# Three 768x768 projections under a max, computed as one level of Strassen's algorithm

## The chip, the cores and the metric

The kernel runs on one core of a Trainium2 chip. The metric is device time in microseconds (us) of one execution, as the median of several runs. PE is the matrix engine (PEld its weight load), DVE the vector engine, ACT the scalar engine, POOL the general-purpose engine, and SP the engine whose queue issues every DMA here.

## The reference

Attention for 2 batches of 12 heads (448 positions, head size 64) with capped scores, a first feed-forward block with a rational activation, and a second one whose hidden layer is the largest of three projections:

```python
attn_out = softmax(cap * tanh(q @ k.T / 8 / cap)) @ v          # 2 x 12 x 448 x 64
x = attn_out.transpose(0, 2, 1, 3).reshape(896, 768)
h = x @ w_in                                                    # 896 x 2048
g = (a0 + a1*h + a2*h*h + a3*h**3) / (1 + |b0|*|h| + |b1|*h*h + 1e-6)
y = g @ w_out                                                   # 896 x 768
m = max(max(y @ w1, y @ w2), y @ w3)                            # three 768 x 768 weights: the change is here
out = m @ w_out2                                                # 896 x 768
```

The weights arrive as 64-bit floats. Every large product is made of three matmuls in single precision with rounded operands (fp32r): a value is split into a rounded high part and the rest as a low part, and high x high, high x low and low x high are summed in PSUM.

## The kernel before

**Layout.** Features lie on the 128 partitions and tokens in the free dimension, one batch (448 tokens) at a time. `y` is six slices of 128 features, each with its two batches; a branch weight is 6 x 6 blocks of 128 x 128. There are 51 SBUF slots of 128 x 2 x 448 fp32 (`NSLOT`) for nearly all data: a weight's decoded form, its high part and its low part take a slot each, and so does a high and low pair of an activation for 448 tokens. There are 3 buffers for raw weights, 4 row buffers, and 8 PSUM banks.

**Stages.** Attention, then `up` (the first product) mixed with the first half of `down` (line 756), which makes three slices of `y` for both batches in six accumulator banks (`acc`); then the second half of `down`, which makes the other three slices in six banks again; then the branches; then `output` (line 904). `finish_x2` (line 783) splits an accumulator of `y` into high and low, negated as the activation leaves it: a copy on ACT and a subtraction on DVE.

**Branches.** `branches(oc, b)` runs for 6 slices of output features and 2 batches. For each of the three weights it adds up 6 x 3 = 18 matmuls of 128 x 448 in a bank. ACT or DVE copies the first bank out (L874), DVE takes the maximum with the second (L879) and the third (L884), ACT rounds the result to the high part (L889), and DVE subtracts for the low part (L894). In all 6 x 2 x 3 x 18 = 648 matmuls.

**Weights.** `weight` (line 391) serves one 128 x 768 stripe: a DMA of 768 KB into a raw buffer, a scaling on ACT or POOL (`scale`, L400, L402), a shift on DVE (L406), `rest`, the lowest bits, on DVE (L425) or ACT (L422), `sign` on DVE (L415), then the high part as a copy on ACT or DVE (L441) and the low part as a subtraction on DVE or POOL (L430). The 18 stripes of the three branch weights are `decm`, `whm` and `wlm` in the trace, those of the second half of `w_out` `decob`, `whob`, `wlob`, and the 6 stripes of `w_out2` `deco`, `who`, `wlo`.

**Who decides the order.** The kernel hands operations with cost estimates to a planner, `Flow` (lines 71 to 283), which plays the program through on its own clock and writes out a fixed order for each engine. PE operations are due in the order in which they are added; every other operation is due early enough for those that need it, and an engine takes the ready operation with the earliest due time whose slots, rows and banks are free. An operation with several engines goes to the first named, unless that is so far behind that another ends sooner. Operations marked `shared` are never put on DVE while POOL works, and POOL takes one only if DVE has enough other work meanwhile. `ahead` and `leave` limit how early slots are taken for weights: the scaling must leave 4 slots free, the high part is made at most 40 us ahead.

Of the kernel before, what the change touches and what calls it, by code (L numbers as in the profile page):

```python
# [18 lines left out]
P = 128  # L19
# [266 lines left out]
def f32(ap):  # L286
    return ap.bitcast(F32)
# [3 lines left out]
def attention_moe(ctx: ExitStack, tc: tile.TileContext, qk, v, w_in, w_out, w123, w_out2, par, out):  # L291
# [96 lines left out]

    weights = {}

    def weight(key, src):
        w = weights[key] = Weight()
        kn = "".join(str(x) for x in key)
        raw, dec, lo, hi = Val("raw", f"raw{kn}"), slot(f"dec{kn}"), slot(f"wl{kn}", F32R), slot(f"wh{kn}", F32R)
        w.hi, w.lo = hi, lo
# [13 lines left out]

        def sign(e):
            t = flat(dec).bitcast(I32)
            mask = -0x80000000 if s3.on == "dve" else -0x7FFFFFF9
            dve.scalar_tensor_tensor(  # L415
                out=t, in0=raws[raw.at[0]][:, :, 1], scalar=mask, in1=t, op0=ALU.bitwise_and, op1=ALU.bitwise_or
            )

        def rest(e):
            if e == "act":  # L420
                byte = raws[raw.at[0]].bitcast(U8).rearrange("p n t -> p (n t)")
                act.activation(byte[:, 4::8], byte[:, 3::8], AF.Copy, scale=1 / 32, bias=-31 / 64)  # L422
# [6 lines left out]
        def low(e):  # L429
            engine[e].tensor_tensor(out=flat(lo), in0=flat(dec), in1=f32(flat(hi)), op=ALU.subtract)  # L430
# [9 lines left out]
        s5 = add(  # L440
            {"act": 0.74, "dve": 0.47}, lambda e: copy_on[e](flat(hi), flat(dec)), [s4], [dec, hi],  # L441
            shared=True, leave=KEEP, ahead=LATE,
        )
        w.done = add({"dve": 0.88, "pool": 1.8}, low, [s5], [dec, lo, hi], shared=True)

    def w_hl(w):
        return flat(w.hi), flat(w.lo)
# [16 lines left out]
        weight(("oa", j), w_out[0, j])  # L464
    for j in range(NFC // 2):
        weight(("ob", j), w_out[1, j])
    for oc in range(NCC):
        for m in range(3):
            weight(("m", oc, m), w123[oc, m])
    for oc in range(NCC):  # L470
        weight(("o2", oc), w_out2[oc])

# [283 lines left out]
    def down(which, n, half):  # L756
# [4 lines left out]
        for o in range(3):  # L761
# [14 lines left out]

            users.append(add({"pe": 3 * MM}, products, [w.done, h_, l_], [a, w.hi, w.lo, hi, lo]))
            if half and len(users) == 1:
                X2[b, o][1].before(users[0])

    X2 = {}

    def finish_x2(b, o):
        half, oo = divmod(o, 3)
        a, users = acc[half, oo, b]
        x = slot(f"x2{b}_{o}", F32R)
# [10 lines left out]
        h_ = add({"act": 0.43}, high, users, [a, x])  # L797
        X2[b, o] = x, add({"dve": 0.54}, low, [h_], [a, x])


    for d in range(B * ND):
# [21 lines left out]
    for k in range(NK):  # L823
# [3 lines left out]
            up(2 * (k + LAG) + 1)  # L827
        down("oa", 2 * k, 0)
        down("oa", 2 * k + 1, 0)
    for b in range(B):  # L830
        for o in range(3):
            finish_x2(b, o)
    for k in range(NK):
        down("ob", 2 * k, 1)
        down("ob", 2 * k + 1, 1)
    for b in range(B):
        for o in range(3):
            finish_x2(b, 3 + o)


    H3 = [(slot(f"h3h{oc}", F32R), slot(f"h3l{oc}", F32R), []) for oc in range(NCC)]

    evac = []

    def branches(oc, b):
        outs, deps = [], []
        for m in range(3):
            o = Val("h", f"m{oc}_{b}_{m}")
            outs.append(o)
        ranges = ((0, 3), (3, 6)) if (oc, b) == (0, 0) else ((0, 6),)  # L850
        last = [None] * 3
        for lo, hi in ranges:
            for m in range(3):
                w, o = weights["m", oc, m], outs[m]

                def products(e, w=w, o=o, lo=lo, hi=hi):
                    whl = w_hl(w)
                    for cc in range(lo, hi):
                        x = two(X2[b, cc][0])
                        for i, (w_, x_) in enumerate(three(whl, slice(cc * P, cc * P + P), (x[:, 0], x[:, 1]))):  # L860
                            pe.matmul(bank(o)[:, :S], w_, x_, start=cc == 0 and i == 0, stop=cc == NCC - 1 and i == 2)  # L861

                xs = [X2[b, cc] for cc in range(lo, hi)]
                last[m] = add(
                    {"pe": 3 * MM * (hi - lo)}, products, [w.done, last[m]] + [x[1] for x in xs],
                    [o, w.hi, w.lo] + [x[0] for x in xs],
                )
        if len(evac) > 1:
            evac[-2].before(*last)
        t = slot(f"t{oc}_{b}")  # L870
        hi, lo, dones = H3[oc]
        cols = slice(b * S, b * S + S)
        c0 = add(
            {"act": 0.43, "dve": 0.54}, lambda e: copy_on[e](two(t)[:, 0], bank(outs[0])[:, :S]), [last[0]],  # L874
            [outs[0], t],
        )
        c1 = add(
            {"dve": 0.54},
            lambda e: dve.tensor_tensor(out=two(t)[:, 1], in0=bank(outs[1])[:, :S], in1=two(t)[:, 0], op=ALU.max),  # L879
            [last[1], c0], [outs[1], t],  # L880
        )
        c2 = add(
            {"dve": 0.54},
            lambda e: dve.tensor_tensor(out=two(t)[:, 0], in0=bank(outs[2])[:, :S], in1=two(t)[:, 1], op=ALU.max),  # L884
            [last[2], c1], [outs[2], t],
        )
        evac.append(c2)
        c3 = add(
            {"act": 0.47, "dve": 0.30}, lambda e: copy_on[e](flat(hi, NT)[:, cols], two(t)[:, 0]), [c2],  # L889
            [t, hi], shared=True,  # L890
        )
        dones.append(add(
            {"dve": 0.54, "pool": 1.1},
            lambda e: engine[e].tensor_tensor(  # L894
                out=flat(lo, NT)[:, cols], in0=two(t)[:, 0], in1=f32(flat(hi, NT)[:, cols]), op=ALU.subtract
            ),
            [c3], [t, hi, lo], shared=True,
        ))

    for oc in range(NCC):  # L900
        for b in range(B):
            branches(oc, b)

    def output(t):
        tk = slice(t * P, t * P + P)
# [4 lines left out]
        for half in range(2):  # L910
            o = Val("h", f"o{t}_{half}")
            ck = slice(half * NH, half * NH + NH)

            def products(e, o=o, ck=ck):
                terms = []
                for oc in range(NCC):
                    hi, lo = (flat(H3[oc][z], NT)[:, tk] for z in range(2))
                    wh, wl = w_hl(weights["o2", oc])
                    terms += [(hi, wh[:, ck]), (hi, wl[:, ck]), (lo, wh[:, ck])]
                for i, (h_, w_) in enumerate(terms):  # L920
                    pe.matmul(bank(o)[:, :NH], h_, w_, start=i == 0, stop=i == len(terms) - 1)  # L921

            ws = [weights["o2", oc] for oc in range(NCC)]
            done = add(
                {"pe": 18 * MO}, products, [w.done for w in ws] + [h[2][b] for h in H3 for b in halves],
                [o] + [x for w in ws for x in (w.hi, w.lo)] + [x for h in H3 for x in h[:2]],
            )
# [64 lines left out]
```

## Time and profile before

| | |
|---|---|
| median of 3 runs | 521.94 us (521.74 to 524.34) |
| profiled execution: its time, its span | 524.37 us, 522.6 us |
| PE busy | 510.7 us (98%), 2637 matmuls |
| DVE busy | 358.8 us (69%) |
| ACT busy | 295.1 us (56%) |
| POOL busy | 47.4 us (9%) |

The shares are means over the whole span; the stages differ. Times in the rows below are us from the start of the span unless marked ns. Neighbouring matmuls overlap in the records, as do neighbouring DVE instructions, so the pace of a run is read from the starts and not from the durations.

### The profile page before, as it was taken

The page shows a single profiled execution, that of the slowest core. Times are in us where ns is not written, and L with a number is a line of the kernel's source. Part 1 is how long each engine was busy: PE and PEld are TensorE (multiplying, and loading weights), DVE is VectorE, ACT ScalarE, POOL GpSimd, SP SyncE. Part 2 cuts the span into 40 slices and gives each one's busy share as a digit, 9 for nine tenths or more (in the row PEclk, how much of TensorE's full clock was granted, in tenths as well). Part 3 has the DMA queues.
Part 4 walks back from the last instruction along what each step waited for, and adds up shares of the span by engine and source line. Part 5 has one row for each costly group of instructions (what it writes and reads, how often), then busy time and mean ns, then how long its engine had stood idle before and what let it go on. Part 6 is the DMA issues. An engine that isn't in the chain of part 4 may idle for free.

```text
span 522.6 us, 6706 instructions
## 1 busy us (share of the span) xinstructions
PE 510.7 (98%) x2637; PEld 418.0 (80%) x2637; DVE 358.8 (69%) x494; ACT 295.1 (56%) x407; POOL 47.4 (9%) x48
## 2 busy tenths in 40 slices
PE   8899999997999999999999999999999999999997
PEld 5333333676899889999997999999999999999996
DVE  0267999989999998788899999999842417111000
ACT  6999999956778866466766553474621121101111
POOL 0202303001201120101010200100000000000000
PEclk9999999999899999999999999999999999999999
DMA  8956755344101112000013678768400000000211
GB/s 308 365 181 217 243 180 212 111 156 154 62 0 61 60 61 60 1 1 2 1 61 99 217 251 279 249 210 271 176 0 2 0 1 0 1 0 10 80 64 61
DMA packets 16448, 58.37 MB, mean 112 GB/s; under 512 B 3592, under 2 KB 6944, under 8 KB 16416
## 3 DMA queue, kind: packets, MB, share of 16 engines
q1 hardware_dynamic: 16416, 57.94, 32.4%
q8 instruction: 20, 0.33, 0.3%
q14 instruction: 12, 0.10, 0.1%
HBM read 55.10 MB, written 2.84 MB: 111 GB/s over the span
## 4 chain that ended last, share of the span: by engine, by line
PE 60%; DVE 18%; DMA 9%; ACT 8%; issue 2%; SPq 2%; DVEq 0%; ACTq 0%
PE b L861 25%; PE b L773 16%; PE b L666 11%; PE b L921 8%; ACT e L536 4%; DMA rsum<-comp 3%; ACT e L539 3%; DMA row<-rsum 3%; SPq L343 2%; DVE W L697 2%; DMA comp<-sums 2%; DVE W L700 2%; DVE W L728 2%; DVE T L725 2%; DVE W L731 1%
## 5 line engine op out<-in xcount | busy, mean ns | idle before, releaser
L861 PE MATMUL b<-x,whm 128*128 128x448 f32 x432 | 122.6, 365 | 0.0
L666 PE MATMUL b<-x,whin 128*128 128x448 f32 x384 | 112.4, 373 | 2.7 <-DVE x L646 1.4
L861 PEld LDWEIGHTS b<-x,whm 128*128 128x128 f32 x432 | 81.1, 188 | 6.4
L666 PEld LDWEIGHTS b<-x,whin 128*128 128x128 f32 x384 | 72.4, 190 | 14.2 <-issue 3.0
L861 PE MATMUL b<-x,wlm 128*128 128x448 f32 x216 | 78.9, 365 | 0.0
L666 PE MATMUL b<-x,wlin 128*128 128x448 f32 x192 | 71.2, 371 | 0.0
L536 ACT ACTIVATE e<-b,qscale 128x448 f32<-128x448 f32 x84 | 49.0, 811 | 2.3 <-PE b L515 2.3
L889 ACT CAST h3h<-t 128x448 fp32r<-128x448 f32 x12 | 6.8, 567 | 66.8 <-DVE t L884 66.7
L539 ACT ACTIVATE e<-e,con 128x896 f32<-128x896 f32 x42 | 44.3, 1249 | 0.0
L861 PEld LDWEIGHTS b<-x,wlm 128*128 128x128 f32 x216 | 40.6, 188 | 3.2
L666 PEld LDWEIGHTS b<-x,wlin 128*128 128x128 f32 x192 | 36.5, 190 | 3.6
L773 PE MATMUL b<-gl,whoa 128*128 128x448 f32 x96 | 35.5, 369 | 2.2 <-DVE gl L748 2.2
L773 PE MATMUL b<-gh,wloa 128*128 128x448 f32 x96 | 35.2, 367 | 0.0
L773 PE MATMUL b<-gh,whoa 128*128 128x448 f32 x96 | 35.2, 367 | 0.0
L773 PE MATMUL b<-gh,whob 128*128 128x448 f32 x96 | 35.2, 366 | 0.0
L515 PE MATMUL b<-qk 64*128 64x448 f32 x144 | 33.6, 564 | 1.6 <-ACT e L536 1.4
L773 PE MATMUL b<-gh,wlob 128*128 128x448 f32 x96 | 35.1, 365 | 0.0
L773 PE MATMUL b<-gl,whob 128*128 128x448 f32 x96 | 35.1, 365 | 0.0
L686 ACT ACTIVATE W<-b,con 128x448 f32<-128x448 f32 x32 | 23.0, 719 | 18.6 <-PE b L666 18.5
L879 DVE TENSOR_TENSOR t<-b,t 128x448 f32<-128x448 f32 x12 | 7.5, 622 | 33.9 <-PE b L861 33.8
L515 PEld LDWEIGHTS b<-qk 64*128 64x128 f32 x144 | 14.3, 186 | 20.1 <-ACT e L536 9.5
L575 PE MATMUL b<-e,v 128*64 128x448 f32 x144 | 29.0, 545 | 0.0
(111 smaller groups left out, 917.7 us busy)
## 6 DMA issues: line engine op xcount, KB each, us to landing
raw<-in_w_out_dram SPq DMA_DIRECT2D x22, 768.0 KB, 4.4
raw<-in_w_dram SPq DMA_DIRECT2D x18, 768.0 KB, 4.2
raw<-in_w_in_dram SPq DMA_DIRECT2D x16, 768.0 KB, 6.0
qk<-in_qk_dram SPq DMA_DIRECT2D x12, 448.0 KB, 7.7
v<-in_v_dram SPq DMA_DIRECT2D x6, 448.0 KB, 11.9
row<-rsum SPq DMA_DIRECT2D x24, 112.0 KB, 3.6
out_dram<-ob SPq DMA_DIRECT2D x6, 384.0 KB, 2.8
out_dram<-ob SPq DMA_DIRECT2D x2, 192.0 KB, 1.9
```

Source lines behind the costliest of these rows:

```text
L343: return add({"sp": issue}, lambda e: nc.sync.dma_start(out=out_(), in_=in_()), after, vals, size=size, **kw)
L515: pe.matmul(pair(t, j)[:, :S], k[rr], q[rr], start=True, stop=True)
L536: act.activation(two(x)[:, j], pair(t, j)[:, :S], AF.Tanh, scale=qscale)
L539: act.activation(two(x), two(x), AF.Exp, scale=cap)
L575: pe.matmul(bank(o)[j * D : j * D + D, :S], whole(vr, n, r, j), two(x)[:, j], start=False, stop=n == NFULL - 1,)
L666: pe.matmul(bank(h)[:, :S], w_, x_, start=cc == 0 and i == 0, stop=cc == NCC - 1 and i == len(terms) - 1)
L686: act.activation(two(w_)[:, i], bank(h)[:, :S], AF.Identity, bias=a2, scale=a3)
L697: dve.tensor_tensor(out=two(w_)[:, i], in0=bank(h)[:, :S], in1=two(w_)[:, i], op=ALU.mult)
L700: dve.scalar_tensor_tensor(out=two(w_)[:, i], in0=two(w_)[:, i], scalar=a1, in1=bank(h)[:, :S], op0=ALU.add, op1=ALU.mult)
L773: pe.matmul(bank(a)[:, :S], w_, g_, start=count[half, o, b] == 1, stop=count[half, o, b] == 3 * NFC)
L861: pe.matmul(bank(o)[:, :S], w_, x_, start=cc == 0 and i == 0, stop=cc == NCC - 1 and i == 2)
L921: pe.matmul(bank(o)[:, :NH], h_, w_, start=i == 0, stop=i == len(terms) - 1)
```

## The change

The branch weights, the `y` of both batches and the result are each seen as 2 x 2 blocks: output features 0-383 and 384-767, contraction halves 0-383 and 384-767, and the two batches. Seven half-size products per weight replace eight (Winograd's form of Strassen's algorithm). `o` = 0, 1, 2 stands for the output slices `o` and `o` + 3, and with 3 weights (`m`) there are 9 sets; a set has 7 products of 3 x 3 = 9 matmuls of 128 x 448, so 567 matmuls in all. Sums of weight blocks are formed before the split into high and low, and sums of products after, in fp32.

`branch_weights` decodes two stripes (`top`, `bot`), combines their halves with four 384-wide additions or subtractions, and splits three and a half stripes in place of two: a set then occupies seven slots (`h1`, `l1`, `h2`, `l2`, `h3`, `l3`, `x4`). `finish_near` and `finish_far` make seven split operands for each of 3 feature slices (`B11`, `T1`, then `T2`, `T3`, `T4`, `B21`, `B22`) out of the accumulators, where there were four. `branches(n)` adds seven banks into four corners with `put`; the maximum is then taken in SBUF (`most`) for the second and third weight. The first two products of the first two sets need only the near half and are put first. For the first two token tiles `output` is cut into two pieces, output slices 0, 1, 3, 4 and then 2, 5.

```diff
@@ weight() is cut into decoded() (up to sign), split() and weight(); the steps of decoded() are unchanged
+    def split(dec, at, n, hi, hat, lo, lat, after):
+        def high(e):
+            copy_on[e](flat(hi)[:, hat : hat + n], flat(dec)[:, at : at + n])
+        def low(e):
+            engine[e].tensor_tensor(
+                out=flat(lo)[:, lat : lat + n], in0=flat(dec)[:, at : at + n], in1=f32(flat(hi)[:, hat : hat + n]),
+                op=ALU.subtract,
+            )
+        f = n / DM
+        s5 = add({"act": 0.1 + 0.64 * f, "dve": 0.07 + 0.4 * f}, high, after, [dec, hi], shared=True, leave=KEEP, ahead=LATE)
+        return add({"dve": 0.06 + 0.82 * f, "pool": 0.1 + 1.7 * f}, low, [s5], [dec, lo, hi], shared=True)
...
+    def branch_weights(o, m):
...
+        def combine(out_, x, y, op, after):
+            (o_, oc), (x_, xc), (y_, yc) = out_, x, y
+            return add(
+                {"dve": 0.47, "pool": 0.95},
+                lambda e: engine[e].tensor_tensor(out=flat(o_)[:, oc], in0=flat(x_)[:, xc], in1=flat(y_)[:, yc], op=op),
+                after, [o_, x_, y_], shared=True,
+            )
...
+        s1 = combine((sd, first), (bot, first), (bot, second), ALU.add, [b4])
+        s2 = combine((sd, second), (sd, first), (top, first), ALU.subtract, [s1, t4])
+        s3 = combine((bot, first), (top, first), (bot, first), ALU.subtract, [s1, t4])
+        d1 = split(top, 0, DM, h1, 0, l1, 0, [t4])
+        d3 = split(sd, 0, DM, h3, 0, l3, 0, [s1, s2])
+        d2 = split(bot, 0, DM, h2, 0, l2, 0, [s3])
+        s4 = combine((top, second), (top, second), (sd, second), ALU.subtract, [d1, s2])
+        d4 = split(top, NH, NH, x4, 0, x4, NH, [s4])
...
-    for oc in range(NCC):
+    for o in range(3):
         for m in range(3):
-            weight(("m", oc, m), w123[oc, m])
+            branch_weights(o, m)
...
+    def from_bank(name, o, a, after):       # as finish_x2: high on ACT, low on DVE, both out of PSUM
...
+    def from_slot(name, o, t, i, after):
+        x = slot(f"{name}_{o}", F32R)
+        h_ = add(
+            {"act": 0.47, "dve": 0.30}, lambda e: copy_on[e](two(x)[:, 0], two(t)[:, i]), after, [t, x], shared=True,
+        )
+        def low(e):
+            engine[e].tensor_tensor(out=two(x)[:, 1], in0=two(t)[:, i], in1=f32(two(x)[:, 0]), op=ALU.subtract)
+        XB[name, o] = x, add({"dve": 0.54, "pool": 1.1}, low, [h_], [t, x], shared=True)
...
+    def finish_near(o):
+        (a0, u0), (a1, u1) = acc[0, o, 0], acc[0, o, 1]
+        t = slot(f"near{o}")
+        c = add({"act": 0.43}, lambda e: act.activation(two(t)[:, 1], bank(a1)[:, :S], AF.Copy, scale=-1.0), u1, [a1, t])
+        b11 = from_bank("B11", o, a0, u0)
+        t1 = add(
+            {"dve": 0.54},
+            lambda e: dve.tensor_tensor(out=two(t)[:, 0], in0=bank(a0)[:, :S], in1=two(t)[:, 1], op=ALU.add),
+            [c, *u0], [a0, t],
+        )
+        evacuated[0, o], evacuated[1, o] = (b11, t1), (c,)
+        near[o] = t, c, t1, from_slot("T1", o, t, 0, [t1])
+
+    def finish_far(o):
...
+        t2 = add({"dve": 0.6}, lambda e: less(two(y)[:, 0], a1, two(t)[:, 0]), [t1, *u1], [a1, t, y])
+        t3 = add({"dve": 0.6}, lambda e: less(two(y)[:, 1], a1, two(t)[:, 1]), [c, *u1], [a1, t, y])
+        from_slot("T2", o, y, 0, [t2])
+        from_slot("T3", o, y, 1, [t3])
+        t4 = add({"dve": 0.6}, lambda e: less(two(t)[:, 0], a0, two(y)[:, 0]), [t2, split1, *u0], [a0, t, y])
+        from_bank("B21", o, a0, u0)
+        from_bank("B22", o, a1, u1)
+        from_slot("T4", o, t, 0, [t4])
...
+    PARTS = {
+        1: ("A11", "B11"), 2: ("A12", "B21"), 3: ("S4", "B22"), 4: ("A22", "T4"), 5: ("S1", "T1"), 6: ("S2", "T2"),
+        7: ("S3", "T3"),
+    }
+    def product(n, i):                      # 3 slices x 3 terms into one bank; waits for the readers 7 products back
...
+    def put(n, i, out_, x, after, vals):    # DVE: out = bank of product i + x
...
+    def branches(n):
+        o, m = SETS[n]
+        for i in (1, 6, 7, 5, 4, 2, 3):
+            product(n, i)
...
+        c1 = add({"act": 0.43, "dve": 0.54}, lambda e: copy_on[e](u1(), bank(first)[:, :S]), [p1], [first, u])
+        e2 = put(n, 6, u2, u1, [c1], [u])
+        e3 = put(n, 7, u3, u2, [e2], [u, third])
+        e4 = put(n, 5, u2, u2, [e3], [u])
+        if m:
+            e22 = put(n, 5, lambda: rows[v.at[0]], u3, [e3], [third, v])
+            e21 = put(n, 4, u3, u3, [e22], [third])
+            e11 = put(n, 2, u1, u1, [e2], [u])
+            e12 = put(n, 3, u2, u2, [e4], [u])
...                                         # most: four maxima in SBUF, DVE; for m == 0 the four sums go to the corners
+    for n in range(2):
+        product(n, 1)
+        product(n, 5)
+    for n in range(len(SETS)):
+        branches(n)
...
+            parts_ = ((0, 1, 3, 4), (2, 5)) if t < 2 else (tuple(range(NCC)),)
```

## Rows read from the trace of the kernel before

**Rows 1.** The chain that ended last: start us, us, engine, written tile, line.

```profile
283.77 59.88 PE b L773 x293
343.64 131.33 PE b L861 x648
474.97 43.72 PE b L921 x252
```

**Rows 2.** Busy time of each engine by stretch.

```profile
core 0: us, PE busy (x) PEld busy (x) DVE busy (x) ACT busy (x) POOL busy (x), PEclk, DMA share, GB/s
90.00:185.00 95.00, 91.17 (x445) 75.46 (x444) 92.15 (x125) 71.66 (x95) 15.11 (x13) 0.98 0.26 88
...
303.00:343.60 40.60, 40.60 (x202) 37.63 (x201) 38.40 (x51) 20.27 (x24) 2.92 (x2) 1.00 0.81 265
343.60:390.00 46.40, 46.40 (x231) 42.99 (x230) 38.79 (x55) 24.84 (x31) 0.00 (x0) 1.00 0.46 158
390.00:475.00 85.00, 85.00 (x422) 78.77 (x421) 25.74 (x38) 11.73 (x20) 0.00 (x0) 1.00 0.00 1
```

**Rows 3.** Waits after 283 us: engine, line, releaser, us in total, times, longest.

```profile
DVE t L879 <- PE b L861: 33.8, 8, 5.5
DVE t L884 <- PE b L861: 24.5, 9, 3.0
```

**Rows 4.** Timeline of DVE, decoding and splitting: start us, us, line, instruction.

```profile
306.16 0.95 DVE L430 TENSOR_TENSOR wlob<-decob,whob 128x768 fp32r<-128x768 f32 x1
307.03 0.95 DVE L415 SCALAR_TENSOR_TENSOR decm<-raw,decm 128x768 int32<-128x768 int32 x1
307.90 0.55 DVE L406 TENSOR_SCALAR decm<-decm 128x768 int32<-128x768 int32 x1
308.49 0.96 DVE L425 SCALAR_TENSOR_TENSOR decm<-raw,decm 128x768 int32<-128x768 int32 x1
309.36 0.95 DVE L430 TENSOR_TENSOR wlm<-decm,whm 128x768 fp32r<-128x768 f32 x1
```

**Rows 5.** Timeline of DVE, 448-wide instructions.

```profile
387.46 0.62 DVE L884 TENSOR_TENSOR t<-b,t 128x448 f32<-128x448 f32 x1 [2.95 <-PE b L861]
388.00 0.95 DVE L430 TENSOR_TENSOR wlm<-decm,whm 128x768 fp32r<-128x768 f32 x1
...
342.74 2.74 DVE L792 SCALAR_TENSOR_TENSOR x<-b,x 128x448 fp32r<-128x448 f32 x5
...
111.29 0.61 DVE L705 TENSOR_TENSOR T<-T,A 128x448 f32<-128x448 f32 x1
111.82 0.95 DVE L425 SCALAR_TENSOR_TENSOR decin<-raw,decin 128x768 int32<-128x768 int32 x1
```

**Rows 6.** Groups: from 283 us (x16, ACT x6), from 303 to 343.6 us (x12, wlm).

```profile
L425 DVE SCALAR_TENSOR_TENSOR decm<-raw,decm 128x768 int32<-128x768 int32 x16 | 15.3, 957 | 0.5
...
L415 DVE SCALAR_TENSOR_TENSOR decm<-raw,decm 128x768 int32<-128x768 int32 x12 | 11.4, 954 | 0.2
...
L430 DVE TENSOR_TENSOR wlm<-decm,whm 128x768 fp32r<-128x768 f32 x6 | 5.7, 951 | 0.0
...
L422 ACT ACTIVATE raw<-raw 128x768 uint8<-128x768 uint8 x6 | 11.9, 1978 | 0.1
```

**Rows 7.** Timeline of DVE and of POOL from 108.5 us.

```profile
109.21 1.56 DVE L646 TENSOR_TENSOR x<-xu,x 128x448 fp32r<-128x448 f32 x1
...
109.15 1.15 POOL L646 TENSOR_TENSOR x<-xu,x 128x448 fp32r<-128x448 f32 x1 [9.84 <-ACT x L642]
```

**Rows 8.** DMA issues: line, queue, count, KB each, median us to landing.

```profile
raw<-in_w_dram SPq DMA_DIRECT2D x18, 768.0 KB, 4.2
```

More of the change, by code (lines that the diff above doesn't have):

```diff
@@ L389, in attention_moe, with decoded @@
     weights = {}
-    def weight(key, src):
-        w = weights[key] = Weight()
+    def decoded(key, src):
         kn = "".join(str(x) for x in key)
-        raw, dec, lo, hi = Val("raw", f"raw{kn}"), slot(f"dec{kn}"), slot(f"wl{kn}", F32R), slot(f"wh{kn}", F32R)
-        w.hi, w.lo = hi, lo
+        raw, dec = Val("raw", f"raw{kn}"), slot(f"dec{kn}")
         def scale(e):
@@ L439, in weight @@
         s4 = add({"dve": 0.87}, sign, [s3], [raw, dec], shared=True)
[L440 to L444, printed above, removed]
+        return dec, s4
+    def split(dec, at, n, hi, hat, lo, lat, after):
[9 more added lines that the diff above has]
+        return add({"dve": 0.06 + 0.82 * f, "pool": 0.1 + 1.7 * f}, low, [s5], [dec, lo, hi], shared=True)
@@ new lines, in weight @@
+    def weight(key, src):
+        w = weights[key] = Weight()
+        kn = "".join(str(x) for x in key)
+        dec, s4 = decoded(key, src)
+        w.hi, w.lo = slot(f"wh{kn}", F32R), slot(f"wl{kn}", F32R)
+        w.done = split(dec, 0, DM, w.hi, 0, w.lo, 0, [s4])
+    def branch_weights(o, m):
+        kn = f"{o}{m}"
+        top, t4 = decoded(("m", o, m), w123[o, m])
+        bot, b4 = decoded(("m", o + 3, m), w123[o + 3, m])
+        sd = slot(f"sd{kn}")
+        first, second = slice(0, NH), slice(NH, DM)
+        def combine(out_, x, y, op, after):
[5 more added lines that the diff above has]
+            )
+        h1, l1, h2, l2, h3, l3 = (slot(f"m{z}{kn}", F32R) for z in ("h1", "l1", "h2", "l2", "h3", "l3"))
+        x4 = slot(f"mx{kn}", F32R)
+        s1 = combine((sd, first), (bot, first), (bot, second), ALU.add, [b4])
[6 more added lines that the diff above has]
+        d4 = split(top, NH, NH, x4, 0, x4, NH, [s4])
+        weights["m", o, m] = {
+            "A11": (h1, 0, l1, 0, d1), "A12": (h1, NH, l1, NH, d1), "S1": (h3, 0, l3, 0, d3), "S2": (h3, NH, l3, NH, d3),
+            "S3": (h2, 0, l2, 0, d2), "A22": (h2, NH, l2, NH, d2), "S4": (x4, 0, x4, NH, d4),
+        }
@@ L778, in down @@
             if half and len(users) == 1:
[L779 to L786, printed above, removed]
+                for e in evacuated[b, o]:
+                    e.before(users[0])
+    XB = {}
+    def from_bank(name, o, a, after):
+        x = slot(f"{name}_{o}", F32R)
         def high(e):
@@ L795, in low, with less @@
             )
-        h_ = add({"act": 0.43}, high, users, [a, x])
-        X2[b, o] = x, add({"dve": 0.54}, low, [h_], [a, x])
+        h_ = add({"act": 0.43}, high, after, [a, x])
+        XB[name, o] = x, add({"dve": 0.54}, low, [h_], [a, x])
+        return XB[name, o][1]
+    def from_slot(name, o, t, i, after):
+        x = slot(f"{name}_{o}", F32R)
+        h_ = add(
[4 more added lines that the diff above has]
+        XB[name, o] = x, add({"dve": 0.54, "pool": 1.1}, low, [h_], [t, x], shared=True)
+        return XB[name, o][1]
+    near, evacuated = {}, {}
+    def finish_near(o):
[11 more added lines that the diff above has]
+    def finish_far(o):
+        (a0, u0), (a1, u1) = acc[1, o, 0], acc[1, o, 1]
+        t, c, t1, split1 = near[o]
+        y = slot(f"far{o}")
+        def less(out_, a, x):
+            dve.scalar_tensor_tensor(out=out_, in0=bank(a)[:, :S], scalar=-1.0, in1=x, op0=ALU.mult, op1=ALU.subtract)
+        t2 = add({"dve": 0.6}, lambda e: less(two(y)[:, 0], a1, two(t)[:, 0]), [t1, *u1], [a1, t, y])
[6 more added lines that the diff above has]
+        from_slot("T4", o, t, 0, [t4])
     for d in range(B * ND):
@@ L829, in attention_moe @@
         down("oa", 2 * k + 1, 0)
-    for b in range(B):
-        for o in range(3):
-            finish_x2(b, o)
+    for o in range(3):
+        finish_near(o)
     for k in range(NK):
@@ L835, in attention_moe @@
         down("ob", 2 * k + 1, 1)
-    for b in range(B):
-        for o in range(3):
-            finish_x2(b, 3 + o)
+    for o in range(3):
+        finish_far(o)
     H3 = [(slot(f"h3h{oc}", F32R), slot(f"h3l{oc}", F32R), []) for oc in range(NCC)]
[L843 to L866, printed above, removed]
-                )
[L868 to L898, printed above, removed]
@@ L900, in attention_moe, with products @@
-    for oc in range(NCC):
-        for b in range(B):
-            branches(oc, b)
+    SETS = [(o, m) for o in range(3) for m in range(3)]
+    PARTS = {
+        1: ("A11", "B11"), 2: ("A12", "B21"), 3: ("S4", "B22"), 4: ("A22", "T4"), 5: ("S1", "T1"), 6: ("S2", "T2"),
+        7: ("S3", "T3"),
+    }
+    MADE, FIN, R, reads = {}, {}, {}, []
+    def product(n, i):
+        if (n, i) in MADE:
+            return
+        w, x = PARTS[i]
+        o = Val("h", f"p{i}_{n}")
+        hi, hat, lo, lat, done = weights[("m",) + SETS[n]][w]
+        xs = [XB[x, cc] for cc in range(3)]
+        def products(e):
+            for cc in range(3):
+                x_ = two(xs[cc][0])
+                wh, wl = (flat(z)[:, at + cc * P : at + cc * P + P] for z, at in ((hi, hat), (lo, lat)))
+                for i, (w_, m_) in enumerate(((wh, x_[:, 0]), (wh, x_[:, 1]), (wl, x_[:, 0]))):
+                    pe.matmul(bank(o)[:, :S], w_, m_, start=cc == 0 and i == 0, stop=cc == 2 and i == 2)
+        op = add(
+            {"pe": 9 * MM}, products, [done] + [x[1] for x in xs], [o, hi, lo] + [x[0] for x in xs],
+        )
+        if len(reads) > 6:
+            for r in reads[-7]:
+                r.before(op)
+        reads.append([])
+        MADE[n, i] = o, op, reads[-1]
@@ L912, in output, with products @@
             ck = slice(half * NH, half * NH + NH)
[L914 to L927, printed above, removed]
+            done = None
+            parts_ = ((0, 1, 3, 4), (2, 5)) if t < 2 else (tuple(range(NCC)),)
+            for ocs in parts_:
+                def products(e, o=o, ck=ck, ocs=ocs):
+                    terms = []
+                    for oc in ocs:
+                        hi, lo = (flat(H3[oc][z], NT)[:, tk] for z in range(2))
+                        wh, wl = w_hl(weights["o2", oc])
+                        terms += [(hi, wh[:, ck]), (hi, wl[:, ck]), (lo, wh[:, ck])]
+                    for i, (h_, w_) in enumerate(terms):
+                        pe.matmul(
+                            bank(o)[:, :NH], h_, w_, start=ocs[0] == 0 and i == 0,
+                            stop=ocs[-1] == NCC - 1 and i == len(terms) - 1,
+                        )
+                ws = [weights["o2", oc] for oc in ocs]
+                done = add(
+                    {"pe": 3 * len(ocs) * MO}, products,
+                    [done] + [w.done for w in ws] + [x for oc in ocs for b, x in H3[oc][2] if b in halves],
+                    [o] + [x for w in ws for x in (w.hi, w.lo)] + [x for oc in ocs for x in H3[oc][:2]],
+                )
             first = "dve" if half == 0 else "act"
```

53 lines of the change are left out of this document (51 added, 2 removed).

## The prediction

> **What bounds the kernel now.** I read the chain that ended last first: from 283.77 us on it is PE and nothing else, 59.88 us of the second half of `down`, 131.33 us of branches, 43.72 us of output [rows 1]. So in this part every matmul taken away is time, as long as nothing else becomes the last to end. A branch matmul costs 131.33 / 648 = 0.2027 us, an output matmul 43.72 / 252 = 0.1735 us. Then I read the stretches of busy time, for the engine that comes next. DVE is busy 38.40 of 40.60 us just before the branches and 38.79 of the next 46.40, but only 25.74 of the last 85.00 [rows 2]; there it waits for PE's banks [rows 3]. So DVE is nearly full while the branch weights are decoded, and has some 60 us to spare afterwards. The question is whether the change's new DVE work fits into that spare time, and whether it can be put there.
>
> **What goes.** 648 - 567 = 81 matmuls at 0.2027 us: 16.4 us. The branches' PE time falls to 567 x 0.2027 = 114.9 us, 12.8 us a set and 1.82 us a product. The new products have the old shape (128 x 128 by 128 x 448), one weight load each, so the pace stays. The page TensorE: Matmul & The Clock Gate of the Trainium skill (section Back-to-back issue gap) gives an isolated matmul a gap of columns / 2.4 GHz plus 2.5 ns, 189 ns here, so an estimate of 15.3 us for the 81; it also gives a sustained stream a smaller one, 131 ns at 512 columns. The trace is above both, and I use the trace.
>
> **What DVE's work costs.** Neighbouring DVE instructions overlap in the records, so I take starts: a 768-wide step takes 0.87 us (L430, L415, L425) and the shift L406 0.59 [rows 4]; a 448-wide step 0.54 us, from PSUM (L884, then L430 0.54 us later; five L792 in 2.74) and from SBUF (L705) [rows 5]. No row has a 384-wide one: it lies between half a 768-wide step, 0.435, and a 448-wide one, 0.54; the line through both widths gives 0.47, which I take, as 448 is near. ACT's new copies and copies out of banks are priced at nothing: ACT is busy 36.6 of the 131.4 us after 343.6 [rows 2], and a set adds at most four ACT steps.
>
> - *Weights, per set.* Two decodes without `rest` 2 x (0.59 + 0.87), two `rest` 2 x 0.87, four combinations 4 x 0.47, low parts 3 x 0.87 + 0.47: 9.6 us, or 7.9 if ACT takes `rest`. Before it was 2 x 4 steps, 6.4 us. Before, 16 of 18 `rest` went to DVE [rows 6], but then little was ready ahead of them; a planner that sees more DVE work ready gives more to ACT, where one takes 1.98 us. I take half, 8.75 us, and keep both ends.
> - *`y`.* Near: 9 steps in place of 6, 1.6 us more. Far: 3 x 8 = 24 steps, 13.0 us, in place of 3.2.
> - *Sums and maxima.* 63 `put` and 24 `most` at 0.54: 47.0 us, in place of 24 steps, 13.0 us. The 12 low parts of the result stay, 6.5 us.
> - *`w_out2`.* 6 x (0.59 + 0.87 + 0.87) = 14.0 us, plus up to 6 x 0.87; before, much of it fell into spare time, now it comes last. I take 16.6.
>
> **What must be done after the branches begin.** Before, 12 stripes were decoded and 6 split by 343.6 us [rows 6], 12 x 2.33 + 6 x 0.87 = 33.2 us of DVE. Less the 1.6 us for the near half, the same time makes 3.3 sets at 9.6 us or 4.0 at 7.9. Left are 5.7 or 5.0 sets: 54.8 or 39.4 us, 46.8 in the middle. With 13.0 + 47.0 + 6.5 + 16.6 that is 129.9 us (low end 119.9, high end 140.5).
>
> POOL can take some combinations and low parts, and hardly more. One 448-wide subtraction takes POOL 1.15 us, and a DVE instruction with two SBUF operands that ran beside it took 1.56 us in place of about 0.62 [rows 7]. So it saves DVE 0.54 and costs it up to 0.94, unless DVE reads PSUM meanwhile. With DVE full from 90 to 185 us, POOL did 13 instructions in 95 us [rows 2], which over this stage would be about 18. Bounds: nothing, and 18 steps of 0.54, some 10 us; I take 5, since part of those 13 were not DVE's work. The Trainium skill's page SBUF — State Buffer (section Who interferes with whom) speaks against the change here: a DVE instruction with two SBUF inputs contends with POOL reading SBUF. Nearly all the new steps but the sums out of banks are of this kind. If it did not hold, POOL could take all combinations at once, an estimate of 36 x 0.47, 17 us less for DVE; rows 7 agree with the rule.
>
> That leaves 125 us. DVE is never full: 38.40 of 40.60 is 95% [rows 2], 92.15 of 95.00 is 97%; at 96% it is 130 us. Some of it may end behind the last branch product, since the first output pieces (4 x 12 matmuls, 8.3 us) need only four of the six output slices: I allow 6 us. So the branches take about 124 us in place of 131.33: **7.1 us faster**, not 16.4. DVE is then what the branches wait for, by some 9 us.
>
> **Where the wait appears.** First at the start. Six accumulators hold six of eight banks. Four early products (7.3 us) use the two free ones, `c1` on ACT giving back the first product's. The next, product 6, needs a bank, and accumulators come free only when DVE reaches `t4` and the low parts of `B21`, behind the steps for `T2`, `T3` and `T4`: 18 x 0.54 = 9.7 us. PE idles some 2 to 3 us, within the 9. Second at the end: seven slots a set, 21 for split `y` and up to 12 for the result leave 18 of 51 for weights in the last three sets, so a set and a half ahead at most. `w_out2` cannot be decoded before the last set and a half, about 19 us, in which DVE also has some 12 us of sums and maxima. I expect PE to wait some us before the first outputs. Behind a late `put` stand the products that need its bank, seven products later, 12.8 us: the late ones are the weights and not the sums. The raw loads are no limit: one lands in 4.2 us [rows 8], and a set needs two in 12.8 us.
>
> **Rivals.**
> - *All of it hides.* ACT takes every `rest`, POOL saves 10: 110 us for DVE, at 97% 113, within 114.9. The whole 16.4 us are kept: 505.5 us. For it: ACT's idle time. Against: before, ACT took few `rest`, and the slots. Chance of a time under 508: 0.14.
> - *DVE eats the gain.* Few `rest` go to ACT and POOL saves nothing: 136 us at 97% is 140, less 6 is 134 for branches, about 131 if part of `rest` moves; within 2.6 us of before, 522. Chance 0.17.
> - *Slower: slots stop the decoding ahead.* A set in work needs ten slots (`top`, `bot`, `sd` besides its seven), and the split `y` grows to 21 slots just when the sets ahead fill the rest. If only two sets are ready at the start, 7 are left: 66.5 + 7 x 8.75 + 16.6 = 144 us, less 5, at 96% 145, less 6: 139 us, 8 slower, 530 us. It decides from about 2.8 sets ready (131 us). For it: 51 - 27 (split `y` and its two temporaries a slice) leaves 24, three sets and three slots. Against: the slots of finished `down` operands come free in time, and before six pairs were decoded by then. Chance 0.25, from just over 524.5 to 532.
>
> **How the numbers follow.** The profiled execution took 524.37 us, 1.8 more than its span; the runs' median is 521.94, 2.4 lower. 7.1 us off gives 517.3 for the first and 514.8 for the second; the forecast is for a median, **515 us**. Its chance, from 508 to 519.3, is 0.44; its own range 509 to 520. With the rivals the range reaches from 506.5 to 527, leaving out about 1 in 10 on each side. 0.5% is 2.6 us, about what a measurement of this kernel can tell from none: faster 0.14 + 0.44 = 0.58, the same 0.17, slower 0.25.
>
> **What would show it.** Branch matmuls: 567 at 0.203 us if PE is fed. DVE over 95% busy from 283 us to the end of the branches, where it had some 60 us idle; PE's gaps in the branch stage end by DVE's steps, 9 us in sum, 2 to 3 of them within 15 us of the start and the rest towards the outputs. `rest` of the branch weights on ACT about 9 of 18. Wrong would be: PE without gaps (the first rival); or gaps in every set from the second on, of 2 us and more (the last); or PE at a lower granted clock than 1.00 behind such gaps, which has no price here.

## The result and the profile after

The changed kernel takes 508.66 us (507.48 to 510.99, 4 runs) against 522.07 us on the same chip: a ratio of 0.974, 95% interval 0.9693 to 0.9786, 13.4 us less. The forecast was 515 us, range 506.5 to 527.

The profiled execution's span is 509.2 us against 522.6, 13.4 us less as well. Its last part, in the view of the chain that ended last:

```profile
351.21 0.62 DVE near L877
351.88 109.71 PE b L949 x540
461.58 43.72 PE b L1057 x252
```

As in [rows 1] it is PE alone, now with 567 branch matmuls: the 540 behind the last wait took 109.71 us, 0.2032 us each, the old pace. Busy time in two stretches, from the first branch matmul to the first output matmul, and from there to the end of the last one:

```profile
core 0: us, PE busy (x) PEld busy (x) DVE busy (x) ACT busy (x) POOL busy (x), PEclk, DMA share, GB/s
345.10:461.40 116.30, 115.48 (x568) 106.35 (x568) 114.94 (x182) 53.34 (x68) 32.34 (x26) 1.00 0.26 88
461.40:505.35 43.95, 43.89 (x253) 43.55 (x252) 8.58 (x16) 8.69 (x19) 1.77 (x1) 1.00 0.16 59
```

The branches take 116.30 us where they took 131.30 (343.50 to 474.80). DVE was busy 64.6 us in that stage before; now it is busy 114.94 of 116.30 and has 8.58 us left for the outputs. PE still waits only twice, 0.8 us in all:

```profile
PE b L949 <- DVE near L877: 0.6, 1, 0.6
PE b L949 <- ACT u L980: 0.2, 1, 0.2
```

What DVE and its helpers did from 283 us on, by groups:

```profile
L420 ACT ACTIVATE raw<-raw 128x768 uint8<-128x768 uint8 x18 | 35.2, 1985 | 3.9 <-POOL decm L400 3.8
...
L423 DVE SCALAR_TENSOR_TENSOR decm<-raw,decm 128x768 int32<-128x768 int32 x7 | 6.9, 990 | 0.1
...
L443 DVE TENSOR_TENSOR mx<-decm,mx 128x384 fp32r<-128x384 f32 x6 | 4.3, 722 | 0.0
...
L423 DVE SCALAR_TENSOR_TENSOR deco<-raw,deco 128x768 int32<-128x768 int32 x2 | 1.9, 944 | 0.0
...
L471 POOL TENSOR_TENSOR sd<-sd,decm 128x384 f32<-128x384 f32 x3 | 4.0, 1346 | 2.1 <-DVE sd L471 2.0
```

`rest` (L423 on DVE, L420 on ACT) went to DVE for 7 of the 18 branch stripes, where it had been 16 [rows 6], and for 2 of the 6 last ones. POOL took 10 combinations (L471, three of them in the last row) and 6 low parts of these weights.

**Where the 13.4 us are.** Branches and outputs together fell from 175.15 to 160.25 us, 14.9 less. The branches began 1.6 us later than before (345.1 against 343.5), and 0.1 us was gained after the last matmul. The change alone does not fix that start: in the twelve kernels with the changed branches that were profiled it lay between 338.7 and 345.2 us, though PE has the same work in front of it in all of them. Where the 1.6 us come from is not shown. Runs of one kernel differ by up to 8 us (before: 520.15 to 527.89 on one chip). So the experiments are compared by the two stages of their profiles, one profile for each kernel, and a median is given beside them. The medians come from several chips; the kernel before took 522.05 to 524.21 us on them.

### The profile page after: what moved, and what is told of

It is laid out like the page before. It is cut to its first block, busy times and chain, and to the rows that moved or that the text cites. A ratio compares the mean times of both kernels' runs of the same rounds, so it can differ in the third digit from the quotient of the medians.

```text
span 509.2 us, 6779 instructions
## 1 busy us (share of the span) xinstructions
PE 494.1 (97%) x2556; PEld 401.8 (79%) x2556; DVE 415.7 (82%) x605; ACT 323.8 (64%) x436; POOL 80.0 (16%) x73
## 4 chain that ended last, share of the span: by engine, by line
PE 33%; DVE 28%; ACT 8%; issue 5%; DMA 2%; POOL 1%; DVEq 0%; ACTq 0%; POOLq 0%; SPq 0%
PE b L949 22%; PE b L1057 9%; PE b L710 3%; DVE W L744 3%; DVE W L775 3%; DVE W L741 3%; DVE W L772 3%; DVE T L769 3%; DMA raw<-in_w_dram 2%; DVE T L749 2%; DVE gl L792 1%; ACT A L765 1%; DVE decm L413 1%; ACT A L766 1%; DVE decob L413 1%
## 5 line engine op out<-in xcount | busy, mean ns | idle before, releaser
L710 PE MATMUL b<-x,whin 128*128 128x448 f32 x384 | 110.7, 369 | 4.8 <-DVE W L744 2.8
L710 PEld LDWEIGHTS b<-x,whin 128*128 128x128 f32 x384 | 71.3, 188 | 16.0 <-issue 3.9
L949 PE MATMUL b<-T,mh 128*128 128x448 f32 x216 | 61.5, 366 | 0.6 <-DVE near L877 0.6
L420 ACT ACTIVATE raw<-raw 128x768 uint8<-128x768 uint8 x26 | 50.9, 1976 | 3.9 <-POOL decm L400 3.8
L949 PEld LDWEIGHTS b<-T,mh 128*128 128x128 f32 x216 | 40.5, 188 | 4.2 <-DVE near L877 1.0
L949 PE MATMUL b<-T,ml 128*128 128x448 f32 x108 | 39.4, 365 | 0.0
L559 PE MATMUL b<-qk 64*128 64x448 f32 x144 | 35.1, 593 | 2.2 <-ACT e L580 1.4
L749 POOL TENSOR_TENSOR T<-T,A 128x448 f32<-128x448 f32 x13 | 17.2, 1320 | 119.8 <-ACT T L734 104.9
L730 ACT ACTIVATE W<-b,con 128x448 f32<-128x448 f32 x32 | 22.9, 718 | 15.6 <-PE b L710 13.6
L949 PE MATMUL b<-B,mh 128*128 128x448 f32 x108 | 30.8, 366 | 0.2 <-ACT u L980 0.2
```

The source lines that it names most:

```text
L559: pe.matmul(pair(t, j)[:, :S], k[rr], q[rr], start=True, stop=True)
L710: pe.matmul(bank(h)[:, :S], w_, x_, start=cc == 0 and i == 0, stop=cc == NCC - 1 and i == len(terms) - 1)
L730: act.activation(two(w_)[:, i], bank(h)[:, :S], AF.Identity, bias=a2, scale=a3)
L749: engine[e].tensor_tensor(out=two(t_)[:, i], in0=two(t_)[:, i], in1=two(a_)[:, i], op=ALU.mult)
L949: pe.matmul(bank(o)[:, :S], w_, m_, start=cc == 0 and i == 0, stop=cc == 2 and i == 2)
```

## The experiments

Two stages in us: branches (first branch matmul to first output matmul), outputs (to the end of the last matmul), DVE's busy time in each, and the median of the runs. The difference to the changed kernel's sum, 160.25 us, is what a variant costs or gains.

| kernel | branches | outputs | sum | DVE in branches | DVE in outputs | median |
|---|---|---|---|---|---|---|
| before | 131.30 | 43.85 | 175.15 | 64.6 | 1.3 | 522.07 |
| changed | 116.30 | 43.95 | 160.25 | 114.9 | 8.6 | 508.66 |
| fewer_before | 115.00 | 43.85 | 158.85 | 65.1 | 1.3 | 507.87 |
| no_max | 116.50 | 43.85 | 160.35 | 112.9 | 5.9 | 506.19 |
| quarter_more_max | 116.30 | 46.75 | 163.05 | 114.6 | 14.1 | 511.69 |
| double_max | 118.20 | 46.55 | 164.75 | 117.1 | 20.8 | 513.41 |
| triple_max | 116.30 | 60.25 | 176.55 | 115.4 | 34.1 | 523.85 |
| rest_dve | 119.70 | 45.95 | 165.65 | 117.1 | 15.7 | 513.09 |
| no_pool | 115.90 | 45.85 | 161.75 | 115.7 | 11.2 | 507.83 |
| dve_alone | 115.90 | 46.65 | 162.55 | 115.9 | 17.1 | 511.62 |
| no_early | 119.10 | 44.95 | 164.05 | 114.5 | 11.0 | 512.80 |
| four_slots | 116.00 | 43.95 | 159.95 | 111.4 | 13.9 | 508.70 |
| nine_slots | 117.10 | 51.05 | 168.15 | 111.7 | 20.5 | 516.13 |
| no_cut | 115.80 | 50.25 | 166.05 | 113.4 | 10.4 | 510.89 |

My theory after the result: PE sets the pace of the branches, and DVE's added work just fits beside and behind it. The rivals: DVE sets the pace, as the prediction had it, or DVE has slack that its busy share hides.

**The removal alone.**

```diff
+                            if (cc == 2 and i) or (cc == 3 and i == 1 and oc < 3 and not b):
+                                continue
                             pe.matmul(bank(o)[:, :S], w_, x_, start=cc == 0 and i == 0, stop=cc == NCC - 1 and i == 2)
```

> The kernel before with 81 of its 648 branch matmuls left out (their terms are missing from the sums) and nothing added: the removal alone. If PE's time is the whole saving, 81 x 0.2027 = 16.4 us less than before, about 505.6 us, and the changed kernel's 508.7 has paid some 3 us for its additions, of which 0.8 are PE gaps at the start of its branches. If the changed kernel's saving came from elsewhere too, this one stays above 508 us.

The two stages took 158.85 us, 16.3 less than before. The removal is the whole saving, and the changed kernel pays 1.4 us of it for all its additions. PE's two waits above are all of that: counted from the starts of the matmuls around them, they cost 1.4 us, and every other matmul keeps the pace. The median, 507.87 us, is above the 505.6 expected; the kernel before took 523.88 us on that chip, 16.0 more.

**Less DVE work.**

```diff
-                    {"dve": 0.54},
-                    lambda e: dve.tensor_tensor(out=y(), in0=x(), in1=y(), op=ALU.max), after, [r, val], shared=True,
+                    {"dve": 0.10},
+                    lambda e: dve.tensor_tensor(out=y()[:, :32], in0=x()[:, :32], in1=y()[:, :32], op=ALU.max), after,
+                    [r, val], shared=True,
```

> The changed kernel with the SBUF maxima taken over 32 of 448 columns only (the rest of the maximum is left out): about 24 x 0.43 = 10 us less DVE work. If PE sets the pace of the branches and DVE only just keeps up: at most 1.5 us faster than 508.7. If DVE sets the pace, as the prediction had it: 5 us faster or more, 503 or less.

160.35 us in the two stages: nothing gained, so DVE does not set the pace. (The median is 2.5 us lower, more than the 1.5 expected; in this profile the branches began at 338.7 us, 6.4 earlier than in the changed kernel's.) DVE is still busy 112.9 us of 116.5 with some 10 us less to do, because the planner took back work that it had given away: its sum over both stages fell by only 4.7 us. The lowest bits on ACT, which were 18 from 283 us on:

```profile
L420 ACT ACTIVATE raw<-raw 128x768 uint8<-128x768 uint8 x13 | 25.6, 1988 | 3.9 <-POOL decm L400 3.8
```

So a DVE that is 97% busy under this planner is no sign that PE waits for it.

**More DVE work.** Each maximum done twice or three times in a row (`for _ in range(2)` or `range(3)` around it), or only one of a set's four:

> The changed kernel with one of the four SBUF maxima of a set done twice: 6 x 0.54 = 3.2 us more DVE work. If DVE has the 3 us to spare that its last results for the first token tiles show: under 1 us slower. If it has none: about 2 to 3 us slower.

> The changed kernel with each of the 24 SBUF maxima done twice: 24 x 0.54 = 13 us more DVE work, same result. DVE is idle 1.4 us in its 116.5 us of branches, and its last result for the first token tiles came about 3 us before PE needed it. If DVE just fits: 13 - 1.4 - 3, so 8 to 10 us slower, about 518. If DVE has slack that its busy share hides (work done early only because it could be): under 3 us slower.

> The changed kernel with each SBUF maximum done three times: 26 us more DVE work, same result. 13 us more cost 4.5 us from the start of the branches to the last output matmul, 164.75 in place of 160.25, with DVE finishing 20.8 us of its work behind the branches. If about 8.5 us is all that DVE's work can end later without PE waiting, the next 13 cost their full length: 177 to 178 us for the two stages. If the helpers keep taking a share of any new work (ACT and POOL): about 169.

The first 13 us cost 4.5, less than the 8 to 10 expected, and some 2.3 of that is not DVE's doing: from 360 to 460 us PE is busy throughout at a granted clock of 1.00 in double_max as in the changed kernel, but starts fewer matmuls, one in 0.2067 us and not in 0.2027 (567 x 0.004 = 2.3 us). The changed kernel's row comes first, double_max's second:

```profile
360.00:460.00 100.00, 100.00 (x495) 92.66 (x494) 99.32 (x153) 45.32 (x53) 28.51 (x22) 1.00 0.26 87
360.00:460.00 100.00, 100.00 (x486) 90.81 (x485) 99.48 (x155) 37.68 (x46) 31.59 (x22) 1.00 0.25 87
```

At equal pace the first 13 us cost about 2.2 and the next 13 about 14, their full length, as triple_max's first expectation had it. The branches themselves do not grow by DVE's work; it moves behind them. With 8.6 us there PE waits for nothing, with 20.8 it loses 2.7 us, with 34.1 it loses 16.3.

The amount behind the branches does not decide alone. The 3.2 us of a quarter cost 2.8 us, as if DVE had nothing to spare, while four_slots below ends with the same 14 us behind the branches and no wait. What PE waits for is the last low parts of the first batch, and there the two differ: in quarter_more_max they ended 9.3 us after the outputs began, and PE's order needs them in the 39th output matmul; in four_slots they ended 7.5 us after, and PE needs them in the 51st. PE in quarter_more_max, then the low parts on DVE in it and in four_slots:

```profile
465.78 0.44 PE L1059 MATMUL b<-who,h3l 128*128 128x384 f32 x1 [1.50 <-DVE h3l L1026]
...
464.58 1.15 DVE L1026 TENSOR_TENSOR h3l<-r,h3h 128x448 fp32r<-128x448 f32 x2
...
466.10 1.15 DVE L1025 TENSOR_TENSOR h3l<-r,h3h 128x448 fp32r<-128x448 f32 x2
```

In triple_max PE's waits are 11.6 us of the 16.3; most of the rest is a lower granted clock behind them. The longest wait ends with a sum (`row`, L964), which points to a bank that this sum had still to read; that is not shown further. PE's waits, and three stretches of the outputs:

```profile
PE b L1059 <- DVE row L964: 6.1, 1, 6.1
PE b L1059 <- ACT h3h L1021: 3.6, 1, 3.6
PE b L1059 <- DVE h3l L1026: 1.9, 2, 1.5
```

```profile
457.80:470.00 12.20, 4.58 (x25) 3.94 (x23) 12.20 (x21) 2.96 (x5) 0.00 (x0) 0.92 0.00 0
470.00:480.00 10.00, 7.15 (x27) 6.83 (x27) 10.00 (x19) 0.00 (x0) 0.00 (x0) 0.76 0.00 0
480.00:490.00 10.00, 8.86 (x41) 8.54 (x42) 10.00 (x20) 5.30 (x12) 0.00 (x0) 0.83 0.21 80
```

**The helpers.**

```diff
-        s3 = add({"dve": 0.87, "act": 1.6}, rest
+        s3 = add({"dve": 0.87} if key[0] in ("m", "o2") else {"dve": 0.87, "act": 1.6}, rest      # rest_dve, dve_alone
...
-                {"dve": 0.47, "pool": 0.95},
+                {"dve": 0.47},                                                                   # no_pool, dve_alone
...
+        on = {"dve": 0.06 + 0.82 * f} if dec.name.startswith(("sd", "decm", "deco2")) else {... "pool": 0.1 + 1.7 * f}
```

> The changed kernel with the step for the lowest bits of the branch and last weights allowed on DVE alone: the 15 of 24 that ACT did return to DVE, 15 x 0.87 = 13 us. If ACT's help is what kept DVE from becoming the bound: 8 to 11 us slower, 517 to 520. If not: within 2 us of 508.7.

> The changed kernel with combinations and low parts of the branch and last weights kept off POOL: 16 steps return to DVE, 10 + 3 of 384 columns at 0.47 us and 3 of 768 at 0.87, 8.7 us. If POOL's steps were a net help: 4 to 7 us slower, 513 to 516. If they cost DVE as much by contention as they save it (its 384-wide steps of 0.55 us averaged 0.62 to 0.89 in the branches): within 2 us of 508.7.

> The changed kernel with the lowest bits, the combinations and the low parts of the branch and last weights on DVE alone: neither ACT nor POOL helps. Apart, the two limits cost 5.4 and 1.5 us in the two stages. The prediction's case in which DVE eats the gain had this. If the helpers' shares add up: 7 us or more, 167 to 172 us for the two stages, where before had 175.15 and 16.4 less would be 158.8. If either alone had already used up the cover behind the branches: more, 172 to 177, and the gain is gone.

rest_dve lost 5.4 us, half of what was expected; 3.4 of it in the branches, by one wait of PE of 2.9 us for `t4` (L877) at their start and a lower clock behind it. The wait comes from another order of the steps there: ACT copied the first product out of its bank 10.4 us after the branches began, where in the changed kernel it was 3.5 us, so there the third product waited for an accumulator, and here the fourth. no_pool lost 1.5 us: sixteen steps fewer on POOL, 8.7 us by their starts, and DVE's total grew by only 3.4 us (126.9 against 123.5). Two more `rest` went to DVE there and four more of the result's low parts to POOL, which nearly cancel (2 x 0.87 and 4 x 0.54). DVE's other steps grew shorter. The 384-wide low parts on DVE, from 345 to 470 us in the changed kernel:

```profile
L443 DVE TENSOR_TENSOR mx<-decm,mx 128x384 fp32r<-128x384 f32 x3 | 2.7, 894 | 0.0
```

The 894 ns are the mean of two at 0.54 and 0.55 us and one at 1.59, beside this subtraction of POOL's:

```profile
403.80 1.59 DVE L443 TENSOR_TENSOR mx<-decm,mx 128x384 fp32r<-128x384 f32 x1
...
403.12 1.85 POOL L443 TENSOR_TENSOR ml<-decm,mh 128x768 fp32r<-128x768 f32 x1 [11.72 <-DVE h3l L1024]
```

With POOL kept off these steps, in the same stretch of no_pool:

```profile
L443 DVE TENSOR_TENSOR mx<-decm,mx 128x384 fp32r<-128x384 f32 x6 | 3.3, 544 | 0.0
```

In both kernels every DVE step of these stages that took over 0.06 us longer than is usual for its shape ran beside a POOL instruction; together they were 6.8 us longer in the changed kernel and 3.2 in no_pool. So some 3.6 us of POOL's 8.7 were cancelled by the time it took from DVE, as [rows 7] had it. That agrees with the Trainium skill's page SBUF — State Buffer (section Who interferes with whom), by which a DVE instruction with two SBUF inputs contends with POOL's reads. The remaining 1.7 us between 8.7 and 3.4 are not accounted for.

dve_alone refutes both of its expectations: in these steps the two helpers together are worth 2.3 us, less than ACT's share alone had seemed to be, since its start has no long wait. DVE then has 133.0 us of work, 115.9 in the branches and 17.1 behind them, and PE loses 2.8 us in the outputs. (POOL still took five 448-wide low parts there, 5 x 0.54 = 2.7 us of DVE's.)

**The start.** Without the early list (`for n in range(2): product(n, 1); product(n, 5)` removed):

> The changed kernel without the list that puts the first and fifth product of the first two sets ahead; the sets' own order is left. If those products are what covers the splits of the far half: two products fewer before the first that needs the far half, about 3.6 us more of PE gaps, 512. If the planner finds such products by itself, because it takes any that are ready: within 1 us of 508.7.

3.8 us slower, 2.8 in the branches and 1.0 in the outputs: PE waits 3.1 us for `t4`, so the planner does not find this cover by itself.

**The slots.** `held` slots are added to the first near step and to every product.

```diff
+    held = [slot(f"held{i}") for i in range(4)]        # 9 in nine_slots
...
-            [c, *u0], [a0, t],
+            [c, *u0], [a0, t, *held],
...
-            {"pe": 9 * MM}, products, [done] + [x[1] for x in xs], [o, hi, lo] + [x[0] for x in xs],
+            {"pe": 9 * MM}, products, [done] + [x[1] for x in xs], [o, hi, lo] + [x[0] for x in xs] + held,
```

> The changed kernel with four of the 51 slots held empty from the near half of y to the last product. If slots limit how far DVE works ahead, as the prediction's slower case had it: DVE idles before the last sets and PE waits at the output, 3 us slower or more. If DVE has no time to work further ahead anyway: within 1.5 us of 508.7.

> The changed kernel with nine of the 51 slots held empty from the near half of y to the last product; four held cost nothing (159.95 us for the two stages against 160.25). If slots decide from some point on, as the prediction's slower case had it: DVE idles 5 us or more in the branches and the two stages take 165 us or more. If DVE's time alone limits how far the weights are ahead: under 162.

Four slots less cost nothing, nine cost 7.9 us, with DVE idle 5.4 us in the branches. The limit lies between. Of the 7.9 us, 7.1 are in the outputs, where the prediction expected PE to wait: 3.6 us of waits, mostly for `w_out2`'s split, and a lower clock behind them (0.61 from 468 to 476 us). With nine held:

```profile
PE b L1058 <- DVE wlo L443: 1.9, 1, 1.9
PE b L1058 <- DVE h3l L1025: 0.9, 1, 0.9
PE b L1058 <- ACT who L440: 0.8, 1, 0.8
```

**The end.** With `parts_ = (tuple(range(NCC)),)` for every tile:

> The changed kernel with the first two token tiles of the output in one piece each, so that the first output matmul needs all six output slices of the first batch; the work is the same. In the changed kernel the last of these was ready 5.2 us after the outputs began. If the cut is what hides DVE's tail: a PE wait of 3 to 5 us before the outputs, 163 to 165 us for the two stages in place of 160.25. If the planner moves these steps forward in time: within 1 us.

5.8 us slower, a little more than the 3 to 5 expected: 4.3 us of waits, then a lower clock. So the cut of the first two tiles is what hides DVE's tail. The stretch behind the waits:

```profile
462.00:470.00 8.00, 8.00 (x39) 8.00 (x39) 4.02 (x8) 1.96 (x4) 0.00 (x0) 0.79 0.00 0
```

No variant that does the whole work beats the changed kernel by more than 0.3 us in its two stages.

## Why the prediction was right, and where it was not

**The time.** The direction was right and 508.66 us lies in the stated range, but not by the sum that gave 515: it is below that sum's own range of 509 to 520, and the saving was 13.4 us, where 7.1 were forecast. It is luck that it stayed above the 508 under which it would have been the first rival's: the two stages alone saved 14.9 us, and the branches began 1.6 us late, which no step of the prediction has.

**Right: the removal.** 81 matmuls at the old pace, 16.4 us forecast, 16.3 measured alone.

**Right: the amount of DVE work.** The sum behind the start of the branches was 125 us; DVE was busy 114.9 + 8.6 = 123.5 us. It came out of terms that were off both ways: ACT took more than half of `rest` (11 of 18 and 4 of 6), and POOL's 16 steps, worth 8.7 us by themselves, left DVE by no_pool no more than 3.4 us lighter, where I had taken 5. (The middle of 54.8 and 39.4 is 47.1, not 46.8; the 0.3 us change nothing.)

**Wrong: "DVE is then what the branches wait for, by some 9 us".** PE waits 0.8 us, and all additions cost 1.4. Two allowances in that step were too small. I filled DVE to 96%, between two stretches of before; it reached 114.94 / 116.30 = 99%. And I let 6 us end behind the last branch product, counting the cover of the first four output pieces only; 8.6 us did, with no wait. With these two the same 125 us of work give 125 / 0.99 - 8.6 = 117.7 us for DVE, 2.8 above PE's 114.9, and the forecast would have been 13.6 us. The cover that I left out is that of the second batch: its results are first needed by the fourth token tile, behind three tiles of 36 matmuls, 3 x 36 x 0.1735 = 18.7 us. No run waits for them, not even triple_max with 34.1 us of DVE's work behind the branches; every wait in the outputs of any run falls in their first 54 matmuls. So four_slots can leave 13.9 us there for nothing, while no_pool loses 1.9 us with 11.2, by 1.5 us of waiting for a low part of the first batch.

**The start: right place, too large.** 0.8 us and not 2 to 3. The wait is for `t4`, as forecast, but it is the fourth early product that waits for the bank, not product 6 behind it, and the planner did not put `t4` behind all the splits for `T2` and `T3`. DVE's order there, in the timeline of the changed kernel:

```profile
345.77 1.16 DVE L877 SCALAR_TENSOR_TENSOR far<-b,near 128x448 f32<-128x448 f32 x2
347.47 0.62 DVE L877 SCALAR_TENSOR_TENSOR far<-b,near 128x448 f32<-128x448 f32 x1 [0.54 <-ACT B L832]
348.01 1.68 DVE L851 TENSOR_TENSOR T<-far,T 128x448 fp32r<-128x448 f32 x3
349.61 1.68 DVE L877 SCALAR_TENSOR_TENSOR far<-b,near 128x448 f32<-128x448 f32 x3
351.21 1.67 DVE L877 SCALAR_TENSOR_TENSOR near<-b,far 128x448 f32<-128x448 f32 x3
```

`t4` (`near`) follows directly on `t3`, so the first accumulator is free 6.7 us after the branches began and not after 9.7.

**The end: no wait.** The four slices of the first pieces and their weights were ready, and the first batch's last low parts ended at 466.8 us:

```profile
465.63 1.15 DVE L1024 TENSOR_TENSOR h3l<-r,h3h 128x448 fp32r<-128x448 f32 x2
```

That was 1.2 us before PE needed them. I had counted four first pieces, 48 matmuls, ahead of the second ones. PE's order has three, 36 matmuls, and a low part is needed in the 39th: 461.42 + 38 x 0.1735 = 468.0. ACT's copy of the third finished output, which PE releases when it has done 54 matmuls, and not 66, shows it:

```profile
471.00 0.48 ACT L1072 COPY ob<-b 128x384 f32<-128x384 f32 x1 [0.56 <-PE b L1057]
```

The 3 us to spare in the expectations of double_max and quarter_more_max were too much for the same reason.

**The rivals.** Full hiding is what happened, at 1.4 us from it, but not by its mechanism: ACT did not take every `rest`, and POOL saved little. "DVE eats the gain" had its conditions nearly met in dve_alone, with 133.0 us for DVE where it had 136, and still cost only 2.3 us. The slower case's mechanism shows with nine slots fewer, not with the 51 that there are, and even then the kernel stays faster than before (516.13 us). The signs that I named for DVE as the bound were misleading: DVE over 95% busy held, and means nothing here; the PE gaps were the ones to look at.

## What to carry to other kernels

When work moves from the engine that sets the pace to one beside it, add up the second engine's work and compare it with the stage plus everything that covers its tail: the time until the next stage needs a result counts as room for it. Where a planner can hand work to several engines, an engine's busy share says little about its slack; doing some of its work twice, or leaving some out, says it. Price a helper that slows what it helps by taking it away: here sixteen steps of help were worth some 3.4 us of 8.7. And look for the result that the next stage needs first, not for the amount of work that is left: 14 us behind the branches cost nothing in one order and 2.8 us in another.

## What the runs showed of the hardware that was not expected

**The clock behind a wait.** Waits of a few us can cost more than their length. Behind 4.3 us of waits in no_cut the granted clock was 0.79 for 8 us; for some 3 us of them the output matmuls started every 0.32 us, and then again every 0.17, which makes about 1.6 us more:

```profile
464.61 0.52 PE L1057 MATMUL b<-who,h3l 128*128 128x384 f32 x1
464.93 0.51 PE L1057 MATMUL b<-who,h3h 128*128 128x384 f32 x1
465.25 0.36 PE L1057 MATMUL b<-wlo,h3h 128*128 128x384 f32 x1
465.46 0.33 PE L1057 MATMUL b<-who,h3l 128*128 128x384 f32 x1
465.63 0.33 PE L1057 MATMUL b<-who,h3h 128*128 128x384 f32 x1
```

In triple_max, in the 20 us behind a wait of 6.1 us that ended at 470.0 us, with one of 3.6 us among them, it was 0.76 and 0.83. Such a mean lies between the two levels, 1.2 and 2.4 GHz, so PE ran at the lower one for part of the stretch. It does not follow every time: after the one wait of 2.9 us in rest_dve, which ended at 348.86 us, the clock was 0.70 from 348 to 352 us and 0.87 in the next four, and after 3.1 us in no_early, up to 351.68 us, it stayed at 1.00. The first four microseconds at each, rest_dve first:

```profile
348.00:352.00 4.00, 3.14 (x10) 2.77 (x11) 4.00 (x9) 2.25 (x5) 0.00 (x0) 0.70 0.00 0
```

```profile
352.00:356.00 4.00, 3.81 (x18) 2.89 (x16) 4.00 (x9) 2.79 (x6) 0.00 (x0) 1.00 0.00 0
```

That is part of why rest_dve's branches are 119.70 us and not shorter.

**Two paces at one clock.** Away from the start of the branches and from waits, the same 128 x 448 matmul started every 0.2027 us in every kernel but double_max, and every 0.2067 there, both at a granted clock of 1.00. Earlier stages have both paces: most matmuls of `up` in the kernel before (L666) go at the slower one. What decides between them is open. Over 567 matmuls that is 2.3 us, more than several of the differences in the table, so a pace has to be looked at before a difference of 2 us is put down to a change.
